# The low part of g's last f: from GpSimd behind the masks to VectorE behind x's low parts

## The chip, the cores and the metric

One core of a Trainium2 chip runs the whole program. The metric is the device time of one execution in microseconds, taken as the median of several runs. Engines are named as in the profile: PE is TensorE's matmuls and PEld its weight loads, DVE is VectorE, ACT is ScalarE, POOL is GpSimd, SP is SyncE.

## What must be computed

Top-32 attention over 8 batches, 8 heads, 576 positions and a head width of 64, then a gated product over the 4608 tokens:

```
scores = q @ k.T / 8
attn   = softmax of the 32 largest scores of each row, 0 elsewhere
x      = attn @ v                       # 4608 x 512 after the heads are joined
h      = ((x @ w1) * (x @ w2)) @ w3     # 1024 wide
out    = h @ w_out                      # 4608 x 512
```

All data is float32. The kernel folds `w3 @ w_out` into one matrix `wf` at its start, so that the second half is `g = (x @ w1) * (x @ w2)` and `out = g @ wf`.

## The kernel before

**Slots and blocks.** The attention is cut into 144 slots. A slot is 128 query rows of one pair of heads (or the last 64 rows of two pairs). Twelve slots give x for 384 tokens, a block, and the gated product of a block is computed while the slots of the next block pass. There are twelve blocks; the last one is computed after the loop over slots.

**One iteration.** The loop of line 595 runs over p and does a different stage of several slots in each iteration, in an order that is written out by hand; every engine works through its own instructions in just that order (`keep_in_program_order`). In iteration p:

- VectorE searches the 32 largest scores of slot p (`top32_steps`, line 258): four `tensor_tensor` that fold three thirds of the row into `w`, then rounds of MAX8 and MATCH_REPLACE8. `folded` (line 613) is the last of the four.
- GpSimd makes the edges of slot p - 1 (`edges_of`) and masks its two halves (`mask`, line 298: ScalarE makes a Relu, GpSimd subtracts it from the scores, 128x576 each). The first mask is made to wait for `folded`.
- ScalarE takes the exponentials of slot p - 1 and normalises slot p - 2.
- TensorE turns the weights of slot p - 3, multiplies turned weights by v, and makes scores of coming slots in pairs.
- At odd p the products with v of two slots are split into x's high part (`split_high`, ScalarE, rounds to fp32r) and low part (`split_low`, VectorE, the rest). These stand in `fresh` and are taken in lines 607 to 616, the low parts behind `folded`.

**The gated product.** `moe_steps` (line 386) yields one matmul at a time, and `fill(n)` puts n of them on TensorE: 12 + 12 + 12 in an iteration with odd p, 12 in one with even p (`SHARES`). Each operand is split in a high and a low part, so three matmuls make one product. For each f of 0 to 7 there are twelve matmuls `ab` with w1 and twelve with w2, 128x128x384 each; then for each e of 0 to 3 there are 24 matmuls `eo`, three for each f in order: high weights with g's high part, low weights with g's high part, high weights with g's low part. A block needs 192 + 96 = 288 matmuls, which is 12 iterations; it begins at p = 15, 27, ..., so its `eo` begins at p = 23, 35, ..., 143 in the first `fill` of an iteration.

**Evictions.** What follows a finished `ab` or `eo` (`take_a`, `take_b`, `take_o`) is put off until the next call of `fill`. `take_b` multiplies the two halves on VectorE into `asb`, and its inner `part` writes g's high part on ScalarE and appends g's low part, a GpSimd subtraction, to the list `lows`. `take_lows` empties that list behind the two masks (line 622) and once more after `take_held` (line 632). The last f (f = 7) is finished by the matmuls of an even p, its multiplication and its high part are issued at the end of that iteration, and its low part behind the masks of the next. Outside the loop over slots `behind_masks` is empty and low parts are issued at once.

`x` has three buffers for blocks, g has eight tiles, `asb` and `osb` share two buffers, and the accumulators `ab` and `eo` share two PSUM banks.

Of the kernel before, what the change touches and what calls it, by code (L numbers as in the profile page):

```python
# [9 lines left out]
F32 = mybir.dt.float32  # L10
# [4 lines left out]
ALU = mybir.AluOpType  # L15
# [7 lines left out]
NCC, NFC, NEC = DM // 128, DF // 128, DM // 128  # L23
# [47 lines left out]
def attn_moe(ctx: ExitStack, tc: tile.TileContext, q, k, v, w1, w2, w3, w_out, out, flag, any_missed, general):  # L71
    nc = tc.nc
    pe, act, dve, pool, sp = nc.tensor, nc.scalar, nc.vector, nc.gpsimd, nc.sync
# [37 lines left out]
    if not general:  # L111
        pe, act, dve, pool, sp = (InOrder(tc, e) for e in (pe, act, dve, pool, sp))
# [90 lines left out]
    def load_v(b, hp):  # L203
        vt = kv_p.tile([128, 11 * D], F32, tag="v", name="vt")
        sp.dma_start(vt, at(v, b, hp))
        return vt
# [41 lines left out]
    def new_s():  # L248
        return att_p.tile([128, 2, S], F32, tag="s", name="s", bufs=S_BUFS)
# [123 lines left out]
    def split_low(high, low, whole):  # L373
        dve.tensor_tensor(low, whole, high.bitcast(F32), op=ALU.subtract)

    lows, behind_masks, held, hold = [], [], [], []

    def take_held():
        while held:
            held.pop(0)()  # L380

    def take_lows():
        while lows:
            lows.pop(0)()

    def moe_steps(xs, nb, places, after):
        def take_a(p, asb):
            act.copy(asb[:, :nb], p[:, :nb])

        def take_b(p, asb, gf):  # L390
            whole = asb[:, :nb]
            dve.tensor_tensor(whole, p[:, :nb], whole, op=ALU.mult)

            def part():
                act.copy(gf[:, 0, :nb], whole)
                lows.append(lambda: pool.tensor_tensor(gf[:, 1, :nb], whole, gf[:, 0, :nb].bitcast(F32), op=ALU.subtract))
                if not behind_masks:
                    take_lows()

            held.append(part)  # L400
            if not hold:
                take_held()

        def take_o(p, e):
            def part():
                osb = o_p.tile([128, NB], F32, tag="o", name="osb")
                act.copy(osb[:, :nb], p[:, :nb])
                for place, cut in places:
                    sp.dma_start(place(slice(e * 128, (e + 1) * 128)), osb[:, cut])

            held.append(part)
            if not hold:
                take_held()

        g = []
        for f in range(NFC):
            asb = o_p.tile([128, NB], F32, tag="o", name="asb")
            g.append(late["g"].tile([128, 2, NB], F32R, tag="g", name="g"))
            for i in range(2):
                p = late["mm"].tile([128, 512], F32, tag="mm", name="ab")  # L420
                for c in range(NCC):
                    for n, (w, x) in enumerate(((wh, 0), (wh, 1), (wl, 0))):
                        pe.matmul(
                            p[:, :nb], w[i][:, c * DF + f * 128 : c * DF + (f + 1) * 128], xs[c][:, x, :nb],
                            start=(c == 0 and n == 0), stop=(c == NCC - 1 and n == 2),
                        )
                        if (c, n) != (NCC - 1, 2):
                            yield
                if i == 0:
                    after(lambda p=p, asb=asb: take_a(p, asb))  # L430
                else:
                    after(lambda p=p, asb=asb, gf=g[f]: take_b(p, asb, gf))
                yield
        for e in range(NEC):
            p = late["mm"].tile([128, 512], F32, tag="mm", name="eo")
            for f in range(NFC):
                for n, (i, j) in enumerate(((0, 0), (1, 0), (0, 1))):
                    pe.matmul(
                        p[:, :nb], wf[i][:, f * DM + e * 128 : f * DM + (e + 1) * 128], g[f][:, j, :nb],
                        start=(f == 0 and n == 0), stop=(f == NFC - 1 and n == 2),  # L440
                    )
                    if (f, n) != (NFC - 1, 2):
                        yield
            after(lambda p=p, e=e: take_o(p, e))
            yield
# [107 lines left out]
    def prefetch(n):  # L553
        while waiting and len(fetched) < n:
            src, step = waiting.pop(0)
            fetched.append((fetch(src), step))
# [3 lines left out]
    def warm():  # L560
        entered.append(p)
        if p < 0:
            return
        if fetched and len(entered) % 2 == 0:
            z, step = fetched.pop(0)
            going.append(step(z))
        going[:] = [unit for unit in going if next(unit, "end") != "end"]
        prefetch(WAITING)
# [26 lines left out]
    for p in range(-2, n_slots + 4):  # L595
        h, i, j, l, m = p + 2, p + 1, p - 1, p - 2, p - 3
        if p == 1:
            vts[0, 0] = load_v(0, 0)
            vts[0, 1] = load_v(0, 1)
            vts[0, 2] = load_v(0, 2)  # L600
            vts[0, 3] = load_v(0, 3)
        finder = top32_steps(ss[p], p) if 0 <= p < n_slots else iter(())
        if 0 <= i < n_slots and i not in ss:
            ss[i] = new_s()
            take_scores(ss[i], sts[i], 1)
            take_scores(ss[i], sts[i], 0)
        for part in fresh:
            split_high(*part)
        if 0 <= j < n_slots:
            edges[j] = edges_of(j)  # L610
        if 0 <= l < n_slots:
            add_up(pabs[l][1])
        folded = next(finder, None)
        for part in fresh:
            split_low(*part)
        fresh.clear()
        warm()
        if 0 <= j < n_slots:
            pabs[j] = new_weights()
            for a in range(2):  # L620
                mask(ss[j], edges[j], pabs[j][0], a, folded if a == 0 else None)
        take_lows()
        warm()
        begin()
        if p % 2:
            fill(SHARES[1][0])
            evict()
        next(finder, None)
        if 0 <= m < n_slots:
            turned[m] = take_turned(pabs[m][0], *turn(pabs[m][0], None if ("wide", 0) in late else sts[i][1]))  # L630
        take_held()
        take_lows()
        if 0 <= l < n_slots:
            invert(pabs[l][1])
            normalise(*pabs[l])
        if 0 <= j < n_slots:
            exps(edges[j], *pabs[j], 0)
        warm()
        if p == 3:
            stir(6)  # L640
        fill(SHARES[p % 2][1])
        next(finder, None)
        warm()
        if h not in sts and (not late or h % 2) and h < n_slots:
            score(h, scores)
            scored(h)
        elif h % 2 == 0:
            for n in (h + 1, h):
                if n < n_slots:
                    score(n, lambda *a, n=n: scores_whole(*a, n % 2))  # L650
            for n in (h, h + 1):
                if n < n_slots:
                    scored(n)
            homes[:] = [wide_banks(1)[:, a, SPLIT:] for a in range(2)]
        ahead = "rest" in late and p % 2 == 1 and h < n_slots and h in sts
        if ahead:
            ss[h] = new_s()
            take_scores(ss[h], sts[h], 1)
        if 0 <= j < n_slots:
            exps(edges[j], *pabs[j], 1)  # L660
        if ahead:
            take_scores(ss[h], sts[h], 0)
        if 0 <= m < n_slots:
            if not put_back(m):
                for n in [m - 1, m] if put_back(m - 1) else [m]:
                    b, hps, t = slots[n]
                    ovs[n] = values(of(vts, b), hps, *turned.pop(n), n < m)
                    renew(vts, load_v, n)
        if p == 14:
            stir(9)  # L670
        next(finder, None)
        warm()
        for _ in finder:
            pass
        if p % 2:
            hold.append(True)
        fill(SHARES[p % 2][2])
        hold.clear()
        for d in sorted(ovs):
            b, hps, t = slots[d]  # L680
            n = d // BLOCK
            for hp in hps:
                if (n, hp) not in xs:
                    xs[n, hp] = new_x(n)
            fresh += parts_of([xs[n, hp] for hp in hps], column[group_of[d]], t, ovs.pop(d))
            del ss[d], pabs[d], edges[d], sts[d]
            if (d + 1) % BLOCK == 0:
                starting.append(n)
        if p == 2:
            stir(8)  # L690
        warm()
    take_lows()
    behind_masks.clear()
    begin()
    worst = small.tile([128, B + 1], F32, tag="worst", name="worst", bufs=1)
# [66 lines left out]
```

## Time and profile before

| what | value |
|---|---|
| median of 3 runs | 1239.58 us (1239.02 to 1241.21) |
| the profiled execution's own time | 1238.84 us |
| its span, first to last instruction | 1237.0 us |
| granted TensorE clock, mean | 0.982 |
| GpSimd `g<-asb,g` | 96 times, 97.2 us busy |
| VectorE's largest group, MAX8 | 1152 times, 466.4 us busy |

Busy time of an engine is the time in which one of its instructions was under way. The chain of waits starts at the last instruction and goes back to what released it; a piece of it on one engine means that this engine was what the end waited for at that time. In a row of a timeline `x2` means two instructions of one kind in a row, and the number after the start is the time from the start of the first to the end of the last. Instructions of one engine can overlap a little, so two of them take less than twice the mean of one.

### The profile page before, as it was taken

Reading aid. Unit: us, or ns where it says so; the run is one execution under the profiler, and the core shown is the slowest. Engines: PE = TensorE matmul, PEld = TensorE weight load, DVE = VectorE, ACT = ScalarE, POOL = GpSimd, SP = SyncE. Lnnn points to the kernel's source line nnn. Section 1 sums busy time; section 2 is a strip of 40 time slices with the busy share of each in tenths; the row PEclk is TensorE's granted clock in tenths of the full one; section 3 lists DMA queues with packets and bytes.
Section 4 is the critical chain, followed back from the end, with each engine's and each line's share of the span. In section 5 each row is a group of like instructions: output and inputs, shape, how many; then the busy total and the mean of one; then the engine's idle time right before and its main releaser. Section 6 shows DMA issues by size and latency. Waiting matters only on the chain.

```text
span 1237.0 us, 27384 instructions
## 1 busy us (share of the span) xinstructions
PE 1177.4 (95%) x9427; PEld 1038.2 (84%) x9427; DVE 1132.4 (92%) x3952; ACT 1106.5 (89%) x2233; POOL 695.5 (56%) x877
## 2 busy tenths in 40 slices
PE   4699689999999999999999999999999999999998
PEld 3444469899899899899899899899899899899898
DVE  7999999999999999999999999999999999999510
ACT  5999989999999999999999999999999999999721
POOL 4777765555555555555555555655655655655410
PEclk7899889999999999999999999999999999999999
DMA  8344310101120020111020021101110021000000
GB/s 300 104 151 140 119 60 10 64 29 33 35 76 12 15 83 17 54 36 43 28 75 11 22 74 32 48 23 52 35 57 10 23 73 55 25 14 2 14 14 28
DMA packets 30116, 64.72 MB, mean 52 GB/s; under 512 B 5396, under 2 KB 11540, under 8 KB 29972
## 3 DMA queue, kind: packets, MB, share of 16 engines
q1 hardware_dynamic: 29972, 62.93, 15.8%
q8 instruction: 75, 1.23, 0.4%
q14 instruction: 69, 0.57, 0.1%
HBM read 53.48 MB, written 9.44 MB: 51 GB/s over the span
## 4 chain that ended last, share of the span: by engine, by line
PE 76%; DVE 14%; ACT 5%; POOL 3%; issue 2%; ACTq 0%; POOLq 0%; DVEq 0%
PE ab L60 31%; PE wide L60 27%; PE eo L60 13%; DVE w L60 5%; PE rest L60 4%; DVE top L60 4%; ACT pab L60 3%; POOL pab L60 3%; DVE t L60 2%; ACT s L60 2%; DVE z L60 2%; POOL g L60 1%; PE st L60 0%; DVE wf L60 0%; PE idle L60 0%
## 5 line engine op out<-in xcount | busy, mean ns | idle before, releaser
L60 POOL TENSOR_TENSOR pab<-s,pab 128x576 f32<-128x576 f32 x288 | 404.5, 1426 | 232.1 <-ACT pab L60 150.1
L60 DVE MAX8 top<-w 128x8 f32<-128x192 f32 (+1 forms) x1152 | 466.4, 447 | 0.0
L60 PE MATMUL ab<-x,wh 128*128 128x384 f32 x1536 | 408.2, 347 | 0.6 <-ACT asb L60 0.5
L60 DVE MATCH_REPLACE8 w<-top,w 128x192 f32<-128x192 f32 x864 | 289.9, 344 | 0.0
L60 PEld LDWEIGHTS ab<-x,wh 128*128 128x128 f32 x1536 | 271.4, 188 | 9.4 <-issue 7.1
L60 PE MATMUL ab<-x,wl 128*128 128x384 f32 x768 | 259.9, 338 | 0.0
L60 PE MATMUL eo<-g,wf 128*128 128x384 f32 x1152 | 223.1, 345 | 11.7 <-POOL g L60 10.9
L60 ACT ACTIVATE pab<-pab,edge 128x576 f32<-128x576 f32 x288 | 225.5, 785 | 1.2 <-POOL pab L60 1.2
L60 ACT ACTIVATE pab<-s,edge 128x576 f32<-128x576 f32 x288 | 211.5, 798 | 6.8 <-POOL edge L60 6.7
L60 ACT ACTIVATE pab<-pab,sums 128x576 f32<-128x576 f32 x288 | 210.2, 789 | 7.7 <-DVE sums L60 7.7
L60 PEld LDWEIGHTS eo<-g,wf 128*128 128x128 f32 x1152 | 199.2, 188 | 18.6 <-POOL g L60 14.4
L60 ACT COPY pab<-wide 128x1024 f32<-128x1024 f32 x130 | 132.1, 1016 | 43.4 <-PE wide L60 43.2
L60 DVE TENSOR_TENSOR w<-w,s 128x384 f32<-128x384 f32 x288 | 159.8, 555 | 5.0
L60 PE MATMUL wide<-pab,vt 128*64 128x128 f32 (+1 forms) x2960 | 159.9, 264 | 0.0
L60 PEld LDWEIGHTS wide<-pab,vt 128*64 128x64 f32 x2960 | 144.8, 137 | 15.3 <-issue 15.3
L60 DVE TENSOR_TENSOR w<-s 128x384 f32<-128x384 f32 x288 | 147.1, 552 | 10.4 <-ACT s L60 7.6
L60 PE MATMUL wide<-ident,pab 128*128 128x128 f32 x1040 | 148.9, 273 | 0.0
L60 PEld LDWEIGHTS ab<-x,wl 128*128 128x128 f32 x768 | 144.4, 188 | 0.0
L60 POOL TENSOR_TENSOR edge<-top,coef 128x4 f32<-128x4 f32 x144 | 42.8, 298 | 167.5 <-DVE top L60 167.5
L60 PEld LDWEIGHTS wide<-ident,pab 128*128 128x128 f32 x1040 | 125.6, 140 | 4.3
L60 POOL TENSOR_TENSOR g<-asb,g 128x384 fp32r<-128x384 f32 x96 | 97.2, 1012 | 41.9 <-ACT g L60 41.9
L60 PE MATMUL wide<-kt,qt 64*128 64x384 f32 (+1 forms) x560 | 108.7, 506 | 0.0
(64 smaller groups left out, 1349.4 us busy)
## 6 DMA issues: line engine op xcount, KB each, us to landing
z<-in_w SPq DMA_DIRECT2D x32, 512.0 KB, 3.7
vt<-in_v SPq DMA_DIRECT2D x32, 352.0 KB, 4.4
qt<-in_q SPq DMA_DIRECT2D x40, 256.0 KB, 2.9
kt<-in_k SPq DMA_DIRECT2D x32, 320.0 KB, 3.4
out_t<-osb SPq DMA_DIRECT2D x32, 192.0 KB, 1.9
z<-in_wo SPq DMA_DIRECT2D x8, 512.0 KB, 7.3
out_t<-osb SPq DMA_DIRECT2D x16, 160.0 KB, 3.3
out_t<-osb SPq DMA_DIRECT2D x16, 32.0 KB, 3.1
```

The source lines that it names most:

```text
L60: ins = fn(*args, **kw)
```

## The change

The low part of f = 7 goes into a list of its own, `lasts`, and its subtraction is a VectorE instruction; those of f = 0 to 6 stay on GpSimd. `take_lasts` empties the list behind x's low parts and ahead of the masks, and once behind the loop.

```
-    lows, behind_masks, held, hold = [], [], [], []
+    lows, lasts, behind_masks, held, hold = [], [], [], [], []
+
+    def take_lasts():
+        while lasts:
+            lasts.pop(0)()
...
-        def take_b(p, asb, gf):
+        def take_b(p, asb, gf, last):
...
                 act.copy(gf[:, 0, :nb], whole)
-                lows.append(lambda: pool.tensor_tensor(gf[:, 1, :nb], whole, gf[:, 0, :nb].bitcast(F32), op=ALU.subtract))
+                to, engine = (lasts, dve) if last else (lows, pool)
+                to.append(lambda: engine.tensor_tensor(gf[:, 1, :nb], whole, gf[:, 0, :nb].bitcast(F32), op=ALU.subtract))
                 if not behind_masks:
                     take_lows()
+                    take_lasts()
...
-                    after(lambda p=p, asb=asb, gf=g[f]: take_b(p, asb, gf))
+                    after(lambda p=p, asb=asb, gf=g[f], last=f == NFC - 1: take_b(p, asb, gf, last))
...
         for part in fresh:
             split_low(*part)
         fresh.clear()
+        take_lasts()
         warm()
...
     take_lows()
+    take_lasts()
     behind_masks.clear()
```

## Rows read from the trace of the kernel before

**Rows 1.** The page, busy time, share of the span and instructions of each engine.

```profile
PE 1177.4 (95%) x9427; PEld 1038.2 (84%) x9427; DVE 1132.4 (92%) x3952; ACT 1106.5 (89%) x2233; POOL 695.5 (56%) x877
```

**Rows 2.** The page, the chain that ended last, by engine and by line.

```profile
PE 76%; DVE 14%; ACT 5%; POOL 3%; issue 2%; ACTq 0%; POOLq 0%; DVEq 0%
PE ab L60 31%; PE wide L60 27%; PE eo L60 13%; DVE w L60 5%; PE rest L60 4%; DVE top L60 4%; ACT pab L60 3%; POOL pab L60 3%; DVE t L60 2%; ACT s L60 2%; DVE z L60 2%; POOL g L60 1%; PE st L60 0%; DVE wf L60 0%; PE idle L60 0%
```

**Rows 3.** The chain in order of time, 322 to 340: start us, us, what.

```profile
326.38 1.17 ACT s L60 x2
...
328.65 2.82 POOL pab L60 x2
331.46 0.96 POOL g L60
...
332.47 2.57 PE eo L60 x13
```

**Rows 4.** Waits of the whole run: us in total, times, longest us.

```profile
PEld eo L60 <- POOL g L60: 14.4, 11, 1.9
...
PE eo L60 <- POOL g L60: 10.9, 11, 1.6
```

**Rows 5.** Ten stretches with a beginning of eo: us, busy by engine, clock, DMA.

```profile
234.54:250.80 16.26, 15.38 (x124) 13.83 (x123) 15.90 (x57) 15.09 (x32) 9.42 (x11) 1.00 0.11 31
326.36:342.62 16.26, 15.38 (x123) 13.83 (x123) 15.96 (x56) 15.08 (x31) 9.52 (x12) 1.00 0.10 30
...
sum 163.06, PE 153.75 PEld 138.24 DVE 159.80 ACT 151.61 POOL 95.27; mean PE 15.38 PEld 13.82 DVE 15.98 ACT 15.16 POOL 9.53
```

**Rows 6.** The ten stretches of two iterations that follow those.

```profile
250.80:265.91 15.11, 15.11 (x124) 13.88 (x123) 14.46 (x53) 13.49 (x28) 8.26 (x10) 1.00 0.08 26
...
sum 151.01, PE 151.01 PEld 138.01 DVE 144.10 ACT 134.83 POOL 82.60; mean PE 15.10 PEld 13.80 DVE 14.41 ACT 13.48 POOL 8.26
```

**Rows 7.** Timeline, VectorE, 310 to 356: start us, us, what [idle before].

```profile
310.64 1.02 DVE L60 TENSOR_TENSOR w<-s 128x384 f32<-128x384 f32 x2
...
325.86 1.01 DVE L60 TENSOR_TENSOR w<-s 128x384 f32<-128x384 f32 x2
...
327.92 0.49 DVE L60 TENSOR_TENSOR x<-wide,x 128x128 fp32r<-128x128 f32 x2
...
333.36 1.03 DVE L60 TENSOR_TENSOR w<-s 128x384 f32<-128x384 f32 x2
...
340.48 1.03 DVE L60 TENSOR_TENSOR w<-s 128x384 f32<-128x384 f32 x2
...
343.13 0.49 DVE L60 TENSOR_TENSOR x<-wide,x 128x128 fp32r<-128x128 f32 x2 [0.57 <-ACT x L60]
...
355.68 1.03 DVE L60 TENSOR_TENSOR w<-s 128x384 f32<-128x384 f32 x2
```

**Rows 8.** Timeline, ScalarE and GpSimd, 325 to 334.

```profile
325.97 0.51 ACT L60 CAST g<-asb 128x384 fp32r<-128x384 f32 x1 [0.18 <-DVE asb L60]
...
325.62 0.20 POOL L60 TENSOR_TENSOR edge<-top,coef 128x4 f32<-128x4 f32 x1 [1.12 <-DVE top L60]
...
333.47 0.51 POOL L60 TENSOR_TENSOR edge<-top,coef 128x4 f32<-128x4 f32 x1 [1.06 <-DVE top L60]
```

**Rows 9.** Groups of instructions: GpSimd's g (ns min/median/max), VectorE's fold (mean ns).

```profile
L60 POOL TENSOR_TENSOR g<-asb,g x96: 986/1012/1047, 184.6 to 1216.9; 128x384 fp32r<-128x384 f32 x96
...
L60 DVE TENSOR_TENSOR w<-s 128x384 f32<-128x384 f32 x288 | 147.1, 552 | 10.4 <-ACT s L60 7.6
```

**Rows 10.** Timeline, TensorE and ScalarE, 1159 to 1166, end of the run.

```profile
1159.62 2.57 PE L60 MATMUL eo<-g,wf 128*128 128x384 f32 x13 [1.59 <-POOL g L60]
...
1165.22 0.99 PE L60 MATMUL wide<-pab,vt 128*64 128x128 f32 x14
...
1161.30 1.44 ACT L60 ACTIVATE pab<-s,edge 128x576 f32<-128x576 f32 x2 [0.99 <-POOL edge L60]
1163.26 1.01 ACT L60 COPY pab<-wide 128x1024 f32<-128x1024 f32 x1 [0.52 <-PE wide L60]
```

## The prediction

> **What bounds the kernel now.** I read the busy shares first. TensorE is busy 95% of the span, VectorE 92% and ScalarE 89%, GpSimd only 56% [rows 1]. Shares alone do not say which of the first three sets the pace, so the chain of waits comes next: 76% of it is TensorE, and in its list by line `POOL pab` with 3% and `POOL g` with 1% stand among the TensorE entries [rows 2]. One per cent of the span is 12 us, and `POOL g` is exactly the instruction that the change moves.
>
> Where these pieces stand is seen in the chain in order of time [rows 3]. TensorE runs until 326.38, then the chain leaves it: ScalarE copies scores (and x, and makes the Relu of the next mask), GpSimd masks two halves (2.82 us from 328.65), GpSimd subtracts g's low part (0.96 us from 331.46), and TensorE goes on at 332.47 with `eo`. In the code this is the iteration p = 35 (p = 11 mod 12), where a block's second product `eo` begins: its first twelve matmuls use g of f = 0 to 3, and the 24th needs the low part of f = 7. That f was finished one iteration earlier, its high part was written by ScalarE from 325.97 on [rows 8], but its low part is issued on GpSimd behind the two masks. The list of waits says the same of the whole run: `eo` waits for `POOL g` 11 times, 10.9 us on the matmul side and 14.4 us on the weight side [rows 4]. Eleven is the number of blocks whose `eo` begins while masks are still made; the twelfth begins after the loop.
>
> What it costs is read from stretches of two iterations, from the end of one product with v to the end of the next but one. The ten such stretches with a beginning of `eo` take 163.06 us together, 16.26 us the first of them [rows 5]; the ten that follow directly, with as many matmuls of the gated product, take 151.01 us, 15.11 the first, and in them TensorE is busy from end to end [rows 6]. The difference is 12.05 us, 1.2 us each, at a granted clock of 1.00 in both. So the pace between these places is TensorE's own, and each beginning of `eo` adds a stall.
>
> **The change part by part.** *Removed:* twelve GpSimd subtractions of 1012 ns [rows 9], one of each block's eight. Eleven of them end a TensorE stall. If nothing else is late, a stretch of 16.26 becomes one of 15.11; over ten of them I take 12.0 us.
>
> *Added:* twelve VectorE subtractions, 128x384, both inputs in SBUF, rounded to fp32r on the way out. The trace has no VectorE instruction of just this kind. The nearest is the first step of the search, the same size with both inputs in SBUF: 552 ns in the mean [rows 9], and two of them together 1.03 us [rows 7], so that the second adds 1.03 - 0.55 = 0.48 us to VectorE's queue. I take 0.47 to 0.48. Below, nothing excludes that a part hides in a pause (0); above, GpSimd's own 1.01 us is the farthest row.
>
> *When the moved result is ready.* VectorE subtracts x's low parts at 327.92 for 0.49 us [rows 7], and the new instruction follows, behind the ScalarE write that it needs and that came before ScalarE's x parts in ScalarE's own order. So it waits for nothing new; it starts at about 328.35 and ends near 328.9. TensorE wants it when the 24th `eo` matmul is due, 1.15 us before 332.47, at 331.3. It is 2.4 us early, and nothing of the stall is left. What is queued behind it on VectorE is the search for the 32 largest; who waits for that is GpSimd's edge and then ScalarE's Relu of the next iteration.
>
> *Can VectorE carry it?* Here the sum is close. From fold to fold of the search, a pair of iterations with two `ab` products each way takes VectorE 325.86 - 310.64 = 15.22 us and has no wait in it; the pair with the beginning of `eo` takes 340.48 - 325.86 = 14.62; the next takes 355.68 - 340.48 = 15.20, of which 0.57 is a wait for ScalarE's x, so 14.63 of work [rows 7]. A block is one, one and four: 14.62 + 14.63 + 4 x 15.22 = 90.13 us. TensorE without the stall needs 6 x 15.11 = 90.66. VectorE's reserve is 0.53 us in each block, and the new instruction takes 0.47 of it. It still fits, by a hair; three of the blocks have smaller pieces of x, with more instructions, and there VectorE will run some tenths later than today. Today VectorE is 2.1 us ahead of TensorE behind each stall (its fold at 340.48 against the end of the stretch at 342.62) and 0.5 ahead in front of it (325.86 against 326.36); afterwards it should be 0.5 ahead in both places. What hides the 0.47 us is that lead; were it gone, a block would lose what VectorE is over, and the bound with 1.01 us is 90.13 + 1.01 - 90.66 = 0.5 us in each block.
>
> *Its neighbour on GpSimd.* The trace shows that GpSimd's small operations are longer beside a VectorE instruction with two SBUF inputs: `edge` takes 0.20 us at 325.62 and 0.51 at 333.47, where VectorE's fold has run since 333.36 [rows 7, 8]. The new instruction runs to 328.9 and the first mask starts at 328.65, so I expect that mask up to 0.25 us later. Behind both masks GpSimd has today the 0.96 us of g [rows 3], which goes, so its queue still ends 0.7 us sooner; the mask's reader is ScalarE's Exp, which comes after two copies and two normalisations in ScalarE's order. The Trainium skill, "SBUF — State Buffer", section "Who interferes with whom", goes farther: of a VectorE instruction with two SBUF inputs and a GpSimd instruction that reads SBUF, the one issued first holds the shared port for all of its time and the other is blocked fully. The longer `edge` agrees with it in one direction; no row of the trace has VectorE held by a long GpSimd operation. By that rule the order decides, and it is the first rival below.
>
> *The end of the run.* The eleventh stall is the longest: 1.59 us before the matmul at 1159.62 [rows 10]. It is not gained whole. The product with v that follows at 1165.22 needs ScalarE's copy of the turned weights, begun at 1163.26; that copy stands behind a Relu at 1161.30 that had waited 0.99 us for GpSimd's edge, and so for VectorE's last search [rows 10]. VectorE will be 0.5 to 0.8 later there in relation (its added instruction, and the lead it lost). The Relus end at about 1162.75 today, so the copy could start at 1163.2 to 1163.5 and end 1.01 later, at 1164.2 to 1164.5: the product with v gains 0.7 to 1.0 of the stall. I take 0.7; the bounds are 0 and the full 1.9 us of the weight side. The twelfth block, after the loop, has no wait for g's low part, and gains nothing.
>
> *Sum.* 12.0 + 0.7 = 12.7 us. The profiled execution took 1238.84 us (span 1237.0), so it becomes 1226.1; the median of the runs shown is 0.74 above the profiled one, so 1226.9.
>
> **Rivals.**
> *The masks get in front of the new instruction (slower).* It is decided at one point: whether VectorE starts it before GpSimd starts the first mask. By the rows it does, by 328.65 - 328.35 = 0.3 us, which is little; and both follow the same earlier VectorE multiplication, the mask by way of ScalarE, so they move together. If it came second and were held for both masks, VectorE would lose up to 2.82 us at each beginning [rows 3]: 90.13 + 0.47 + 2.82 = 93.4 us a block against 91.8 now (90.66 + 1.15). Ten blocks make 16 us more, 1255 us. Held for one mask only, 92.0, some 2 us more, 1241. For it speaks the longer `edge`; against it the order in the rows.
> *VectorE sets the pace already (slower).* Then the stall is only a place where TensorE waits for its partner anyway, and eleven times 0.47 us come on top: 1239.6 + 5.2 = 1244.8. For it speak 92% busy and the 14% of VectorE in the chain [rows 1, 2]; against it the wait of 0.57 us and the lead of 2.1 us behind each stall.
> *VectorE becomes the bound after the change.* With 1.01 us for the instruction, or with waits that the lead hides today, each of ten blocks loses 0.5 us of its 1.15: 12.7 - 5 = 7.7 us gained, 1231.9. For it speaks the reserve of 0.06 us that is left; against it that 552 ns is a near row.
> *It does nothing.* Another operand of the same `eo` could be as late: the high part of f = 7 from ScalarE. It was begun at 325.97 [rows 8], five microseconds before its use, so this would need an order that the diff does not show: 1239.6.
>
> **How the numbers follow.** Forecast 77%; VectorE as the new bound, with a partial gain, 11%; masks in front 5%; VectorE as the pace 3%; nothing 4%. What a measurement of this kernel can tell from no change is 0.2%, 2.5 us. Faster by more than that: 77 + 11 = 88%; within: 4%; slower: 8%. The forecast's own range is 1225.0 (the whole last stall, and 0.6 more) to 1229; the partial case reaches to 1233, and with that I leave out little more than the slower cases: 1225.0 to 1233.0.
>
> **What would show it.** The waits of `eo` for `POOL g` are gone; the first stretch with a beginning of `eo` takes 15.1 to 15.2 us; `g<-asb,g` stands 12 times on VectorE with about 550 ns and 84 times on GpSimd; the wait of VectorE's x for ScalarE in the pair after the beginning shrinks to about nothing; the first mask starts up to 0.25 us later behind x. Wrong it would be shown by the new instruction at 1.4 us or more, or behind the mask, by TensorE waits for `ScalarE pab` in place of those for g, or by stretches of `ab` longer than 15.11 us.

## The result, and the profile after

| | median | runs | ratio to before, 95% interval |
|---|---|---|---|
| before | 1239.68 us (1239.02 to 1241.21) | 4 | |
| changed | 1228.45 us (1228.04 to 1229.64) | 4 | 0.9911 (0.9899 to 0.9923) |
| changed, once more, beside other kernels | 1228.76 us (1228.47 to 1229.26) | 5 | 0.9913 (0.9900 to 0.9927) |

The change is 11.2 us faster; 12.7 were predicted. The profiled execution took 1228.37 us, 10.5 less than the one of before.

The page's busy shares and chain, as in [rows 1, 2]:

```profile
PE 1175.3 (96%) x9427; PEld 1038.7 (85%) x9427; DVE 1137.5 (93%) x3964; ACT 1104.7 (90%) x2233; POOL 687.9 (56%) x865
...
PE 71%; DVE 22%; ACT 3%; issue 2%; DMA 1%; SPq 0%; POOL 0%; DVEq 0%; ACTq 0%; POOLq 0%
```

VectorE has twelve instructions more, GpSimd twelve fewer, and `POOL g` is no longer in the chain; VectorE's share of it has grown from 14% to 22%, a first hint of what took the rest of the gain. The instructions that write g's low part (ns min/median/max, first and last start), and the waits of TensorE:

```profile
L60 POOL TENSOR_TENSOR g<-asb,g x84: 989/1012/1040, 185.1 to 1202.2; 128x384 fp32r<-128x384 f32 x84
L60 DVE TENSOR_TENSOR g<-asb,g x12: 548/550/1707, 237.1 to 1206.4; 128x384 fp32r<-128x384 f32 x12
...
PEld ab L60 <- DVE x L60: 2.8, 9, 0.6
```

The 14.4 us of `eo` for `POOL g` [rows 4] are gone from the list. Two things are new: weight loads of `ab` wait for VectorE's x, and one VectorE instruction of the twelve took 1.71 us, not 0.55. Both are part of the loss.

The ten stretches with a beginning of `eo`, against [rows 5] (first, second and sum):

```profile
234.98:250.09 15.11, 15.11 (x123) 13.88 (x123) 14.78 (x55) 14.58 (x32) 7.59 (x8) 1.00 0.10 31
325.84:340.96 15.12, 15.12 (x124) 13.89 (x123) 14.91 (x55) 14.62 (x31) 7.69 (x9) 1.00 0.11 32
...
sum 151.12, PE 151.12 PEld 138.83 DVE 148.20 ACT 146.42 POOL 76.25; mean PE 15.11 PEld 13.88 DVE 14.82 ACT 14.64 POOL 7.63
```

163.06 became 151.12: 11.9 us, and TensorE is busy from end to end. The prediction had 12.0. But the second stretch after each of these, in which the next block's `ab` begins, is longer now. First the ten of before (their sum), then those of the changed kernel (the first, the longest, the sum):

```profile
sum 151.11, PE 151.11 PEld 137.39 DVE 140.84 ACT 143.32 POOL 78.23; mean PE 15.11 PEld 13.74 DVE 14.08 ACT 14.33 POOL 7.82
```

```profile
265.19:280.52 15.33, 15.33 (x123) 13.84 (x123) 15.05 (x55) 14.34 (x30) 8.33 (x13) 1.00 0.10 31
...
719.61:735.18 15.57, 15.32 (x139) 13.54 (x139) 15.30 (x55) 14.33 (x30) 8.62 (x13) 1.00 0.28 98
...
sum 153.35, PE 152.80 PEld 137.42 DVE 150.57 ACT 143.33 POOL 83.56; mean PE 15.28 PEld 13.74 DVE 15.06 ACT 14.33 POOL 8.36
```

That is 2.24 us given back. VectorE's busy time in them went from 140.84 to 150.57: it used to wait there for ScalarE's x, and now TensorE waits for VectorE's. The last of the ten, VectorE and TensorE's matmuls and weight loads (a matmul that is held shows as a longer one, or as a later start):

```profile
1082.99 1.03 DVE L60 TENSOR_TENSOR w<-s 128x384 f32<-128x384 f32 x2
1083.94 1.14 DVE L60 TENSOR_TENSOR w<-w,s 128x384 f32<-128x384 f32 x2
1085.00 0.48 DVE L60 TENSOR_TENSOR x<-wide,x 128x128 fp32r<-128x128 f32 x2
...
1083.74 0.62 PE L60 MATMUL ab<-x,wh 128*128 128x384 f32 x2
...
1084.90 0.88 PE L60 MATMUL ab<-x,wh 128*128 128x384 f32 x2
...
1085.34 0.19 PEld L60 LDWEIGHTS ab<-x,wh 128*128 128x128 f32 x1 [0.42 <-DVE x L60]
```

The same block in the kernel before, where the first `ab` starts at 1093.49:

```profile
1094.39 0.49 DVE L60 TENSOR_TENSOR x<-wide,x 128x128 fp32r<-128x128 f32 x2 [0.79 <-ACT x L60]
...
1094.49 0.43 PEld L60 LDWEIGHTS ab<-x,wh 128*128 128x128 f32 x2
```

The first `ab` of the block starts at 1083.74. Its 8th matmul needs x's low part of chunk 2 (chunk c is the c-th of the four tiles that hold x's 512 columns), which VectorE ends at 1085.28. The matmul's weight load waits for it and starts at 1085.34, 0.06 us behind it and 1.60 us after the first `ab`. In the kernel before, x's low part was ready 1.18 to 1.23 us after the first `ab` in these ten blocks, the weight load started 0.06 us behind it, at 1.24 to 1.28, and the matmul at 1.34. So the load already followed VectorE directly, and there was next to no room: over the ten blocks the 9th matmul comes 2.2 us later than before, which is the loss.

How much of VectorE's lead that takes can be read from the same traces. Count the lead from the start of VectorE's fold to the end of the product with v that opens the stretch. In the kernel before it is 2.01 to 2.06 us at these ten places, and VectorE spends 0.79 us of it waiting for ScalarE's x. In the changed kernel it is 0.67 to 1.09, and each stretch has lost what the lead lacks to some 1.19 us (1.14 in three blocks): 0.22 us in the first, where the fold starts 0.97 us ahead of 265.19, and 0.37 in the last, where it starts at 1082.99 and the stretch 0.82 us later.

The last beginning of `eo`, VectorE and GpSimd, then TensorE's stretch (before, after):

```profile
1146.12 0.48 DVE L60 TENSOR_TENSOR x<-wide,x 128x128 fp32r<-128x128 f32 x2
1146.52 1.71 DVE L60 TENSOR_TENSOR g<-asb,g 128x384 fp32r<-128x384 f32 x1
...
1146.38 3.14 POOL L60 TENSOR_TENSOR pab<-s,pab 128x576 f32<-128x576 f32 x2 [1.63 <-DVE w L60]
```

```profile
1151.88:1167.62 15.74, 13.30 (x107) 12.49 (x107) 9.17 (x31) 13.67 (x30) 8.21 (x12) 1.00 0.05 14
```

```profile
1142.47:1157.22 14.75, 13.26 (x108) 12.53 (x107) 10.80 (x32) 11.60 (x25) 7.55 (x11) 1.00 0.01 2
```

Here the first mask began 0.14 us ahead of the moved instruction, and that took 1.71 us. The stretch became 1.0 us shorter, where 0.7 was predicted. In it the product with v now waits for ScalarE's copy of the turned weights:

```profile
1155.91 1.31 PE L60 MATMUL wide<-pab,vt 128*64 128x128 f32 x20 [0.64 <-ACT pab L60]
```

The account of the two profiles: 11.9 - 2.2 + 1.0 = 10.7; the changed one reached its first such stretch 0.4 us later (234.98 against 234.54), in a part that the change does not touch. That leaves 10.3 of the 10.5 us between them.

### The profile page after: what moved, and what is told of

The parts are those of the page before. It is cut to its first block, busy times and chain, and to the rows that moved or that the text cites. A ratio compares the mean times of both kernels' runs of the same rounds, so it can differ in the third digit from the quotient of the medians.

```text
span 1226.6 us, 27378 instructions
## 1 busy us (share of the span) xinstructions
PE 1175.3 (96%) x9427; PEld 1038.7 (85%) x9427; DVE 1137.5 (93%) x3964; ACT 1104.7 (90%) x2233; POOL 687.9 (56%) x865
## 3 DMA queue, kind: packets, MB, share of 16 engines
q8 instruction: 75, 1.23, 0.4%
## 4 chain that ended last, share of the span: by engine, by line
PE 71%; DVE 22%; ACT 3%; issue 2%; DMA 1%; SPq 0%; POOL 0%; DVEq 0%; ACTq 0%; POOLq 0%
PE ab L60 32%; PE wide L60 25%; PE eo L60 11%; DVE w L60 9%; DVE top L60 7%; PE rest L60 4%; DVE t L60 2%; DVE z L60 2%; ACT pab L60 1%; DVE x L60 1%; ACT s L60 1%; DMA z<-in_wo 1%; DMA vt<-in_v 1%; DVE wf L60 0%; PE st L60 0%
## 5 line engine op out<-in xcount | busy, mean ns | idle before, releaser
L60 PE MATMUL eo<-g,wf 128*128 128x384 f32 x1152 | 220.2, 344 | 0.8 <-ACT asb L60 0.8
L60 POOL TENSOR_TENSOR g<-asb,g 128x384 fp32r<-128x384 f32 x84 | 85.1, 1014 | 36.6 <-ACT g L60 36.6
```

Of the source, the lines that this page charges most:

```text
L60: ins = fn(*args, **kw)
```

## The experiments

After the result I had two theories of the rest. **Mine:** VectorE's extra 0.47 us eats the lead with which it used to have x's low part ready for the next block's `ab`; and beside that, order decides whether the new instruction or the mask holds the other. **The rival:** VectorE as a whole had become the pace, and the place of the wait means nothing. They were timed in two sets of four, each beside the kernel before on one chip, which had 1239.69 us in both.

**The same place, on GpSimd.** The list `lasts` stays, but its engine is GpSimd, and the instruction waits for the fold:

```
-                to, engine = (lasts, dve) if last else (lows, pool)
+                to, engine = (lasts if last else lows), pool
...
-        take_lasts()
+        take_lasts(folded)
```

(`take_lasts(folded)` makes each instruction of the list wait for `folded`.)

> The low part of f = 7 stays on GpSimd, but is issued ahead of the two masks, made to wait for the fold of the next slot as the first mask is. Theory (what was gained is the place ahead of the masks; what was lost again, some 2.2 us at ten beginnings of ab, is x's low part, which VectorE brings later since it has the extra 0.47 us): g's low part is ready about 1 us after the fold, TensorE wants it 2.4 us later, VectorE keeps its old lead, so the 8th ab matmul of a block comes at 1.34 us as before the change, and the eleventh stall is gained without VectorE being held: 1225.6 to 1226.5 us. Rival (GpSimd's 1.01 us ahead of the masks delays them by 0.3 us or more, and the masks' readers miss it): 1229 us or more.

Measured 1225.41 us, ratio 0.9882 (0.9867 to 0.9897): as the theory says, and 3.0 to 3.4 us better than the changed kernel. GpSimd's instruction and masks in one block, and the last stretch:

```profile
328.20 1.01 POOL L60 TENSOR_TENSOR g<-asb,g 128x384 fp32r<-128x384 f32 x1 [1.61 <-DVE w L60]
329.17 2.82 POOL L60 TENSOR_TENSOR pab<-s,pab 128x576 f32<-128x576 f32 x2
```

```profile
1141.13:1155.01 13.88, 13.04 (x107) 12.55 (x107) 9.17 (x31) 12.45 (x26) 8.25 (x12) 1.00 0.04 13
```

GpSimd stood idle for 1.61 us ahead of it. No row of `ab` for VectorE's x is left, the 8th matmul of every block comes at 1.33 or 1.34 us, and the last stretch is 1.86 us shorter than before, the whole stall. VectorE does not keep its old lead, as I had written: with the stall gone it is 1.26 to 1.55 us at the ten beginnings of `ab`, not 2.0. But that is enough, and the ten stretches take 151.21 us, against 151.11 before and 153.35 in the changed kernel.

**Where the 2.2 us are.** In the changed kernel, the first `ab` group of each block uses x's low parts of chunks 2 and 3 in its 11th and 12th matmul:

```
+                steps = [(c, w, x) for c in range(NCC) for w, x in ((wh, 0), (wh, 1), (wl, 0))]
+                if f == 0 and i == 0:
+                    steps = [steps[k] for k in (0, 1, 2, 3, 4, 5, 6, 8, 9, 11, 7, 10)]
...
```

> The changed kernel; in the first ab group of a block alone the twelve matmuls stand in another order: x's low parts of chunks 2 and 3 are used in the 11th and 12th instead of the 8th and 11th. Theory (TensorE stalls for x's low part of chunk 2, which is up to 0.4 us late): three matmuls of 0.18 us are more than that, the stall goes in all ten blocks, 2.2 us, 1226.2 us. Rival (VectorE as a whole is the pace now, and the stall only shows it): the wait comes up elsewhere, 1228.4 us.

Measured 1226.55 us, ratio 0.9891 (0.9876 to 0.9906), 1.9 to 2.2 us better than the changed kernel. The ten stretches with a beginning of `ab` took 15.07 to 15.12 us again, and the row of `ab` for VectorE's x is gone. Their sum, and VectorE's x in the last of them, where the first `ab` starts at 1082.53:

```profile
sum 151.00, PE 151.00 PEld 137.91 DVE 150.00 ACT 143.31 POOL 86.26; mean PE 15.10 PEld 13.79 DVE 15.00 ACT 14.33 POOL 8.63
...
1083.79 0.48 DVE L60 TENSOR_TENSOR x<-wide,x 128x128 fp32r<-128x128 f32 x2
```

VectorE was as late as in the changed kernel: its lead was 0.66 to 1.06 us, and x's low part of chunk 2 ended 1.30 to 1.70 us after the first `ab`. So VectorE's lateness cost only what this one consumer could not wait, and the rival falls. The last block still had its 1.71 us.

**The two on VectorE swapped.** `take_lasts()` stands ahead of x's low parts.

> The changed kernel with the two swapped on VectorE: g's low part of f = 7 first, then x's low parts. Theory (order decides who holds whom): the instruction starts 0.4 us earlier and is done before the first mask starts, in the last block too, where it is now in front: 0.55 us there, not 1.71, and the product with v that follows comes up to 0.9 us earlier; x's low parts of that iteration have time, and the waits at the beginnings of ab stay: 1227.5 us. Rival (the 1.71 us has no part in the end of the run): 1228.4 us.

Measured 1226.74 us, ratio 0.9896 (0.9880 to 0.9911). The direction is right; the size is 0.8 us better than expected. The last beginning of `eo`, VectorE and GpSimd:

```profile
1145.55 0.55 DVE L60 TENSOR_TENSOR g<-asb,g 128x384 fp32r<-128x384 f32 x1
1146.02 0.48 DVE L60 TENSOR_TENSOR x<-wide,x 128x128 fp32r<-128x128 f32 x2
...
1145.81 2.98 POOL L60 TENSOR_TENSOR pab<-s,pab 128x576 f32<-128x576 f32 x2 [1.63 <-DVE w L60]
```

The instruction is in front and takes 0.55 us; this time the masks are longer. The last stretch took 13.90 us, 0.85 less than in the changed kernel. What I had not expected: the waits of `ab` for x fell to four, 1.1 us, and the ten stretches with a beginning of `ab` took 152.10 us, 1.25 less than in the changed kernel. VectorE's lead at the fold that follows two iterations later was 0.60 to 0.63 us here in the first two blocks, 0.42 to 0.53 in the changed kernel. The traces show where those 0.1 to 0.2 us arise, between the start of the fold and the search's first MAX8: 2.86 to 2.87 us here against 2.94 to 2.95, and 2.99 to 3.00 against 3.20 in the four blocks with small pieces of x. A part is a pause ahead of x: in the changed kernel x's first part starts at 327.42, as the fold ends, while a swapped instruction starts 0.1 us before the recorded end of its fold (1145.55 against 1145.63). What causes that pause is not shown.

**One more on VectorE.** The list `lasts` gets the subtraction twice.

> VectorE makes the low part of f = 7 twice, one behind the other, the same values. Theory (after the change VectorE has almost no reserve: 90.13 + 0.47 against 90.66 us a block): another 0.47 us makes 91.07, the wait of the first ab for x's low part grows by 0.4 to 0.5 us in each of ten blocks, 1232 to 1233.5 us. Rival (VectorE still has room, and the loss at the beginning of ab has another cause): 1228.5 us.

Measured 1247.08 us, ratio 1.0059 (1.0045 to 1.0073). The direction is mine, the size is not: +18.6 us, where 4 to 5 were expected. VectorE and GpSimd at one beginning of `eo`, and TensorE's waits:

```profile
330.20 2.25 DVE L60 TENSOR_TENSOR g<-asb,g 128x384 fp32r<-128x384 f32 x2
...
330.52 3.22 POOL L60 TENSOR_TENSOR pab<-s,pab 128x576 f32<-128x576 f32 x2 [2.18 <-ACT pab L60]
...
PE rest L60 <- ACT pab L60: 4.6, 10, 0.5
PE ab L60 <- DVE x L60: 3.6, 10, 0.4
PE rest L60 <- ACT s L60: 3.1, 10, 0.5
```

The second instruction starts when the first mask has begun, and takes 1.66 us in all ten blocks. So the added cost was not 0.47 but 1.6 us a block, which VectorE does not have: its share of the chain of waits is 36%, against 22% in the changed kernel. The ten stretches with a beginning of `eo` took 16.28 to 16.56 us again, and those with a beginning of `ab` 15.71 to 15.73. It is the slower rival of the prediction in action, and it shows how narrow the place is: what starts 0.6 us behind the moved instruction meets the mask in every block.

**Into the masks.** `take_lasts()` of the changed kernel stands behind the second step of the search.

> The low part of f = 7 on VectorE, but issued behind the second step of the search, some 1.2 us later, when GpSimd is in its masks. Theory (with both inputs in SBUF VectorE is held by a GpSimd operation that began first, as it was once in the changed kernel, at 1146.5, where it took 1.71 us): the instruction takes 1.1 to 2.5 us in the blocks, VectorE loses 1 to 2 us more in each, 1240 us or more. Rival (the 1.71 us at 1146.5 had another cause): 0.55 us each, ready before TensorE wants it, 1228.5 us.

Measured 1232.09 us, ratio 0.9940 (0.9925 to 0.9955). Between the two. VectorE and GpSimd:

```profile
329.85 1.00 DVE L60 TENSOR_TENSOR g<-asb,g 128x384 fp32r<-128x384 f32 x1
...
329.00 3.14 POOL L60 TENSOR_TENSOR pab<-s,pab 128x576 f32<-128x576 f32 x2 [2.18 <-ACT pab L60]
```

It was held in ten of eleven, but took only 0.85 to 1.00 us, 0.3 to 0.45 more than alone, since only the rest of the first mask was left; then it went between the two masks, and the second mask took 1.75 to 1.77 us. My 1.1 to 2.5 us had assumed both masks in front. VectorE's lead at the beginnings of `ab` fell to 0.22 to 0.66 us, and those ten stretches took 157.15 us, 3.8 more than in the changed kernel; the last stretch gained its whole stall.

**The instruction without its use.** The kernel before, and VectorE makes the same values in the place of the change, so that TensorE still waits for GpSimd:

```
+                lowered = lambda engine: engine.tensor_tensor(gf[:, 1, :nb], whole, gf[:, 0, :nb].bitcast(F32), op=ALU.subtract)
+                if last and behind_masks:
+                    lasts.append(lambda: lowered(dve))
+                lows.append(lambda: lowered(pool))
...
```

> The kernel before, with the added VectorE instruction beside it: VectorE makes the low part of f = 7 in the place of the change, and GpSimd makes it again behind the masks, the same values, so TensorE still waits for GpSimd. Theory (VectorE leads by 2.1 us behind each stall, and the lead hides 0.47 us; the instruction alone costs nothing as long as the stall is there, but for the last block, where VectorE is held by the first mask for some 1.2 us): 1239.7 to 1240.9 us. Rival (VectorE sets the pace): eleven times 0.47 us more, 1244.9 us.

Measured 1242.06 us, ratio 1.0020 (1.0011 to 1.0029): above my 1239.7 to 1240.9, below the rival's 1244.9. First two stretches with a beginning of `eo`, and GpSimd in the second:

```profile
235.11:251.60 16.49, 15.39 (x124) 13.83 (x123) 16.13 (x58) 15.15 (x32) 9.63 (x11) 1.00 0.11 33
327.16:343.52 16.36, 15.38 (x123) 13.83 (x123) 16.12 (x57) 15.17 (x31) 9.61 (x12) 1.00 0.11 30
...
329.46 2.90 POOL L60 TENSOR_TENSOR pab<-s,pab 128x576 f32<-128x576 f32 x2 [2.18 <-ACT pab L60]
332.31 1.00 POOL L60 TENSOR_TENSOR g<-asb,g 128x384 fp32r<-128x384 f32 x1
```

VectorE's 0.47 us cost nothing by itself: `ab` begins without a wait, x's low part is ready 1.18 to 1.23 us after it, as before, and VectorE's lead there is 1.91 to 2.06 us. Nor does the missing stall by itself, as GpSimd in the same place shows. In the changed kernel it takes both to bring the lead below the 1.19 us. What the ten stretches lost, 0.06 to 0.26 us each, came by way of GpSimd: the masks took 2.90 us, not 2.82 (3.04 in the blocks with small pieces of x), and the g behind them, for which TensorE waits in this kernel, came as much later. I had left that out. The stretches and the last one (16.02 against 15.74 us) make 1.6 of the 2.4 us. The profiled executions lie 2.1 us apart, and this one reached its first such stretch 0.6 us later (235.11 against 234.54), in a part that the edit does not touch.

**GpSimd without the wait for the fold.** As the first one, but `take_lasts()` without `folded`.

> As the version with GpSimd ahead of the masks, but without its wait for the fold of the next slot: it may begin while VectorE is in the fold, whose instructions have two SBUF inputs. Theory (the one that begins first holds the other): GpSimd's 1.01 us gets between two fold instructions, VectorE is held for up to 1 us in each of ten blocks, its lead of 0.5 us is gone, x's low part is late again: 1227 to 1233 us. Rival (they do not hold each other): 1225.4 us.

Measured 1229.62 us, ratio 0.9921 (0.9908 to 0.9935), 4.2 us worse than with the wait. VectorE's fold and GpSimd:

```profile
326.12 1.97 DVE L60 TENSOR_TENSOR w<-w,s 128x384 f32<-128x384 f32 x2
...
325.90 1.18 POOL L60 TENSOR_TENSOR g<-asb,g 128x384 fp32r<-128x384 f32 x1
...
PEld ab L60 <- DVE x L60: 4.7, 10, 0.6
```

GpSimd began between two fold instructions; the next one took 1.37 to 1.38 us, not 0.55, in all eleven blocks, and `ab` waited for x ten times: the ten stretches took 155.12 us, 3.9 more than with the wait. VectorE is held by GpSimd, and not only the other way.

**The changed kernel again.**

> The changed kernel once more on the same chip as the others of this set: 1228.4 us by both theories.

Measured 1228.76 us, as in the table.

## Why the prediction was right, and where it was off

- *TensorE's own pace of 15.11 us and a stall of 1.15 at each beginning of `eo`:* right; 12.0 predicted, 11.9 measured over ten stretches.
- *The price of the instruction:* 0.55 us, with 0.47 added to VectorE's queue, in ten of eleven blocks with masks; it started at 327.83, 0.41 behind x, and nothing held it there.
- *VectorE 0.5 us ahead in both places:* about right, 0.50 and 0.53 at p = 35 and 37; over the ten blocks it is 0.15 to 0.53 in the second place, lowest where x comes in small pieces (four of the ten, not three) and at p = 85. **The step that failed is the next sentence:** "What hides the 0.47 us is that lead". I asked whether VectorE's sum over a block fits and whether the lead is used up, and priced only what VectorE is over in its sum, at most 0.5 us a block and nothing in the forecast. I did not go to the place where an `ab` begins and ask what the lead of 2.1 us paid for there. It paid for x's low part, whose reader, the weight load of a block's 8th matmul, followed it by 0.06 us already. The rows of the kernel before had the answer: VectorE led there by 2.05 us and stood idle for 0.79 of it, so that a lead under some 1.26 us makes x late. By the prediction's own terms the lead would be 0.5 + 15.11 - 14.63 = 1.0 us there, which is an estimate of some 0.3 us lost in each of ten blocks; 0.22 was measured. The other order of the matmuls shows it: with x used later the loss is gone while VectorE is just as late.
- *VectorE as the bound after the change:* the third rival had "waits that the lead hides today" in it, with 0.5 us a block. That mechanism came in beside the forecast's own, at under half of the price. Stretches of `ab` longer than 15.11 us, which the prediction named as a sign of being wrong, were 15.18 to 15.57.
- *The end of the run:* 0.7 predicted, 1.0 measured, but that is luck. The path was the one described: VectorE's search, GpSimd's edge, the Relu, then ScalarE's copy, for which the product with v waits 0.64 us. What made VectorE late was not the 0.5 to 0.8 us that I priced, though. The mask came first, and the instruction took 1.71 us. With the order mended (swapped, or on GpSimd) the copy holds nothing back and the stretch gains the whole 1.85 us, so that for an instruction of 0.55 us the bound of 1.9 was the right size.
- *The masks in front:* given 5%, and it happened in one block of eleven, where ScalarE has no scores to copy and the mask's Relu is early. In the changed kernel, where the moved instruction was first, the first mask did not start later behind x, as I had expected (by up to 0.25 us); it took longer, 1.51 to 1.65 us in place of 1.43. Over the runs a VectorE instruction right behind the start of a mask took 1.66 to 1.71 us in place of 0.55, and a fold instruction behind GpSimd's subtraction 1.37 to 1.38. The rule of the Trainium skill ("SBUF — State Buffer", "Who interferes with whom"), that the one issued first holds the shared port and the other is blocked, agrees with these rows.
- *VectorE as the pace:* refuted by the kernel with the instruction and without its use, which lost 2.4 us and not 5.2, and most of those by way of GpSimd.

So the forecast was 1.5 us too low: one term that it did not have took 2.2 us (`ab` waiting for x), and the end of the run gained 0.3 more than predicted.

## What to carry to other kernels

A stall on one engine can be slack for another. Before you fill it, list who consumes that slack, at the next place where a buffer or a block begins as well as at the stall itself, and look how much room each consumer has: how long the other engine stands idle there, and how soon after its result the reader starts. A sum over the period does not show it. And where an engine with time to spare can do the same work earlier, a change of place can be worth more than a change of engine. Here GpSimd had 1.61 us of idle time, and the kernel was 3.0 to 3.4 us faster with it than with VectorE, but only while its instruction waited for VectorE's fold.

## What was not expected of the hardware

A VectorE subtraction with two SBUF inputs that meets a GpSimd mask in progress does not wait for both masks: it goes between the two, though the second was queued, and then the second mask is held (1.72 to 1.77 us in place of 1.43). In the profile such a hold does not stand as idle time or a wait; it makes the held instruction longer, 0.55 to 1.71 us, so that only the largest of a group's durations shows it.

Open is a pause of 0.46 us on VectorE in the block at p = 85, ahead of its fold at 704.38, which makes that block's wait for x the longest (15.57 us). It came again in the repeat, in the swapped kernel, in the one with matmuls shifted, in the one into the masks and in the one without its use; it did not come with GpSimd, in the kernel before, or with the subtraction made twice. In all six traces that have it, it stands at the same place in the sequence of VectorE's instructions, and the other four have fewer or more instructions ahead of that place. Its cause was not looked for by an experiment.
